# First batch of a block-sparse attention and Fourier-mixing kernel: two units' scores ahead of their two mask matmuls, masks on 64 rows, short steps of the second slot at once

## The chip, the cores and the metric

One core of a Trainium2 chip; the experiments ran on two chips, as said below. The metric is the time of one execution in microseconds (us), as the median of the runs quoted. All runs compared here are in the same, fast state; the one exception is named where it occurs. The clock records of a trace show what share of its full clock PE was granted, in stretches of 3.4 us or multiples of it (3.41, 6.83 and 17.07 us in the kernel before); a stretch at 0.50 is called a *half-clock window*.

The engines are written as the profile writes them: PE (TensorE, matmuls), PEld (its weight loads), DVE (VectorE), ACT (ScalarE), POOL (GpSimd), SP (the queue that starts transfers). Times inside an execution count from its first instruction.

## The reference

```python
# attention: q, k, v of (4, 8, 768, 64); blocks of 32 -> 24 x 24 blocks
scores = scale * np.matmul(q, k.transpose(0, 1, 3, 2))
# mask: band of width 1, first and last block row and column, 3 random blocks per row
scores = np.where(mask, scores, -1000000000.0)
scores = scores - np.max(scores, axis=-1, keepdims=True)
attn = np.exp(scores)
attn = attn / (np.sum(attn, axis=-1, keepdims=True) + 1e-09)
attn_out = np.matmul(attn, v)                 # -> x of (4, 768, 512)

# Fourier mixing and a channel MLP
X = np.fft.fft(np.fft.fft(x, axis=1), axis=2)
u = x + np.real(X).astype(np.float32)
un = (u - mean(u)) / np.sqrt(var(u) + 1e-06)
return u + np.maximum(un @ w_ch1, 0.0) @ w_ch2
```

## The kernel before

A *unit* is one block of 128 keys against 384 queries for two heads, a *slot* is two units, and a batch has 24 slots. In the first batch the mask is added to the scores by a second matmul into the same PSUM tile (written by PE's matmuls; the mask matmul has 24 rows: one for each block); from the second batch on the mask is instead multiplied in on DVE after the exponential. While the first batch runs, ACT and DVE also convert the MLP's weights, 32 *weight rounds* of two ACT and five DVE instructions.

```python
at_k = acc_p.tile([P, 2, 2 * HS], BF16, tag="acc", name="at_k")   # mask operands, bf16
at_q = acc_p.tile([P, 2, 2 * HS], BF16, tag="acc", name="at_q")
of_k, off_q, keep_q = at_k[:, 0, :], at_q[:, 0, :], at_q[:, 1, :]
# ... rows 0:24 and 64:88 are filled (D = 64, NB = 24, HS = 384)

def scores(u):                                    # one unit
    # ... (timing model left out)
    s = ps_s.tile([P, 2, 512], FP32, tag="s", name="s")
    for i in range(2):                            # 64 rows, f32
        nc.tensor.matmul(s[:, i, 0:HS], kT[D * i:D * i + D, c * P:(c + 1) * P],
                         qT[D * i:D * i + D, half * HS:(half + 1) * HS],
                         start=True, stop=n >= NP)
    if n < NP:                                    # first batch: 24 rows, bf16
        for i in range(2):
            nc.tensor.matmul(s[:, i, 0:HS], of_k[D * i:D * i + NB, c * P:(c + 1) * P],
                             off_q[D * i:D * i + NB, half * HS:(half + 1) * HS],
                             start=False, stop=True)
    return s

def w_round(i):                                   # one weight round
    nc.scalar.mul(out=lo.bitcast(FP32), in_=lo, mul=2.0 ** -52)
    nc.scalar.mul(out=a.bitcast(FP32), in_=hi.bitcast(FP32), mul=2.0 ** -112)
    # ... four DVE instructions on a and dst
    nc.vector.tensor_add(out=dst, in0=dst, in1=a.bitcast(FP32))

def slot(sl):
    for u, ps in [(u, scores(u)) for u in units]:
        weigh(u, ps)                              # exp on ACT (second batch: then mask on DVE)
    # ... values of the slot before (o), sums (sp)
    if sl == 1:
        short.append(("t", 0.0, lambda: turn(0, 0, 1)))   # transpose second half of first q
    # ...
    while short and (s in (2, 5) or len(short) > 1 or phase == 0 or r == 0):
        ready = [i for i in short if max(i[1], min(free[i[0]])) <= when["PE"] + 0.1]
        if not ready and s not in (2, 5) and r > 0:
            break                                 # short step left for the next slot
        # ... do one short step
    # ...
    w_steps(sl)                                   # weight rounds due by this slot
```

## Time and profile before

| | before |
|---|---|
| median of 3 runs | 1109.58 us (1108.61 to 1111.27) |
| PE busy | 1065.3 us, 96% of the profiled span |
| first scores of batch 1, of batch 2 | 8.60, 135.41 us |
| scores with their masks, per slot (start to start) | 2.23 us |
| longest wait of PE in batch 1 | 4.04 us, ended at 25.27 by the copies of q on DVE |
| first masked multiply of batch 2 (DVE) | 140.19 us |

A busy PE shows that PE is the engine to save time on; it does not show that every saving arrives. So the rows to look at are those where PE hands over to another engine: the wait at 25.27, and the start of the second batch, where its work waits for DVE. A timeline line reads: start, duration, engine, source line, operation, output <- inputs, shapes, count, and in brackets the idle time before it with what ended it. The prediction shows the lines.

### The profile page before, as it was taken

How to read it: one execution, taken by the hardware profiler on the slowest of the kernel's cores; microseconds unless marked ns; L12 is line 12 of the kernel's file. 1: busy time of each engine (PE TensorE's matmuls, PEld its weight loads, DVE VectorE, ACT ScalarE, POOL GpSimd, SP SyncE). 2: the span in 40 equal slices, each digit the busy share in tenths (PEclk: the TensorE clock that was granted, in tenths of full speed). 3: DMA queues.
4: the chain of work that ended last, by engine and by line, in shares of the span. 5: the costliest groups of instructions: out<-in, count | busy, mean ns of one | idle time of the engine just before them, and what ended most of it. 6: DMA issues, size and time to landing. Idle time of an engine off the chain costs nothing.

```text
span 1108.8 us, 12273 instructions
## 1 busy us (share of the span) xinstructions
PE 1065.3 (96%) x4370; PEld 537.9 (49%) x4370; DVE 670.6 (60%) x1227; ACT 389.8 (35%) x786; POOL 271.2 (24%) x302
## 2 busy tenths in 40 slices
PE   7999988998899999999999999999999999999996
PEld 4333333443455545444444545444444555568675
DVE  5688878497864535564558635555456446575563
ACT  5788755565202102253443212344330202120210
POOL 1000078487200001245537000343540000000000
PEclk9999999999999999999999999999999999999998
DMA  7557322022000000212210000211000000100001
GB/s 237 151 161 234 109 53 59 15 44 43 1 1 1 1 1 19 62 24 39 43 29 15 0 1 1 55 46 29 1 1 1 0 1 20 38 1 1 1 16 44
DMA packets 86689, 44.28 MB, mean 40 GB/s; under 512 B 74318, under 2 KB 79452, under 8 KB 86620
## 3 DMA queue, kind: packets, MB, share of 16 engines
q1 hardware_dynamic: 84732, 42.62, 14.5%
q10 hardware_dynamic: 1856, 0.79, 0.3%
q8 instruction: 36, 0.59, 0.2%
q14 instruction: 33, 0.27, 0.1%
q0 software_dynamic: 32, 0.01, 0.0%
HBM read 37.11 MB, written 6.29 MB: 39 GB/s over the span
## 4 chain that ended last, share of the span: by engine, by line
PE 83%; DVE 10%; ACT 2%; issue 2%; DMA 1%; POOL 1%; SPq 0%; ACTq 0%; DVEq 0%; POOLq 0%
PE y L1017 23%; PE z L961 14%; PE s L541 10%; PE o L585 8%; PE yp L961 7%; PE yy L1080 6%; PE xp L961 3%; DVE e L562 3%; PE zp L774 1%; PE sp L632 1%; PE zp L745 1%; DMA out_dram<-x 1%; PE xt L603 1%; PE tp L483 1%; DVE w_sb L452 1%
## 5 line engine op out<-in xcount | busy, mean ns | idle before, releaser
L572 POOL TENSOR_TENSOR acc<-acc,e 128x384 f32<-128x384 f32 x192 | 197.4, 1060 | 89.5 <-DVE e L562 88.9
L541 PE MATMUL s<-qT,kT 64*128 64x384 f32 x768 | 164.4, 531 | 15.2 <-DVE e L562 11.0
L562 DVE TENSOR_TENSOR e<-s,mask 128x768 f32<-128x768 f32 x144 | 131.1, 949 | 65.0 <-ACT s L560 62.9
L585 PE MATMUL o<-e,vr 128*64 128x384 f32 x768 | 148.0, 507 | 0.0
L560 ACT ACTIVATE s<-s 128x768 f32<-128x768 f32 x144 | 109.5, 791 | 89.3 <-PE s L541 88.1
L1020 DVE TENSOR_TENSOR x<-y,x 128x512 f32<-128x512 f32 x72 | 49.8, 691 | 146.8 <-PE y L1017 146.7
L1017 PE MATMUL y<-w_sb,hA 128*128 128x512 f32 x288 | 129.5, 595 | 1.1 <-ACT zs L776 1.1
L1017 PE MATMUL y<-w_sb,hB 128*128 128x512 f32 x288 | 128.5, 596 | 1.0 <-DVE x L1020 1.0
L572 POOL TENSOR_TENSOR acc<-e 128x384 f32<-128x384 f32 x48 | 50.0, 1063 | 231.3 <-DVE e L562 189.1
L541 PEld LDWEIGHTS s<-qT,kT 64*128 64x128 f32 x768 | 62.4, 187 | 85.1 <-DVE e L562 37.9
L966 DVE TENSOR_TENSOR hA<-z,hA 128x384 f32<-128x384 f32 x64 | 35.7, 558 | 97.5 <-PE z L961 97.5
L961 PE MATMUL z<-unT,t 128*128 128x384 f32 x256 | 93.0, 486 | 0.0
L837 POOL TENSOR_SCALAR st<-st 128x1 f32<-128x1 f32 x24 | 6.7, 277 | 348.1 <-DVE st L836 347.7
L1017 PEld LDWEIGHTS y<-w_sb,hB 128*128 128x128 f32 x288 | 53.3, 190 | 67.3 <-issue 65.6
L585 PEld LDWEIGHTS o<-e,vr 128*64 128x64 f32 x768 | 47.4, 138 | 75.9 <-issue 72.3
L1017 PEld LDWEIGHTS y<-w_sb,hA 128*128 128x128 f32 x288 | 52.9, 190 | 62.9 <-issue 58.5
L970 ACT ACTIVATE hA<-hA 128x384 f32<-128x384 f32 x64 | 33.5, 523 | 119.9 <-DVE hA L966 119.5
L961 PEld LDWEIGHTS z<-unT,t 128*128 128x128 f32 x256 | 48.6, 190 | 33.9
L970 ACT ACTIVATE hB<-hB 128x384 f32<-128x384 f32 x64 | 33.5, 523 | 86.1 <-DVE hB L966 86.1
L961 PE MATMUL xp<-unT,w_sb 128*128 128x384 f32 x128 | 48.5, 503 | 1.3 <-DVE x L1020 0.7
L981 ACT COPY hA<-xp 128x384 f32<-128x384 f32 x32 | 15.3, 479 | 95.8 <-PE xp L961 95.8
L961 PE MATMUL z<-t,w_sb 128*128 128x384 f32 x128 | 46.6, 487 | 0.9 <-DVE t L923 0.9
(197 smaller groups left out, 1409.1 us busy)
## 6 DMA issues: line engine op xcount, KB each, us to landing
wraw<-in_moe_w_ch_dram SPq DMA_DIRECT2D x32, 512.0 KB
vr<-in_v_dram SPq DMA_DIRECT2D x30, 192.0 KB
qr<-in_q_dram SPq DMA_DIRECT2D x48, 64.0 KB
kr<-in_k_dram SPq DMA_DIRECT2D x14, 192.0 KB
qb<-in_q_dram SPq DMA_DIRECT2D x28, 96.0 KB
kb<-in_k_dram SPq DMA_DIRECT2D x28, 96.0 KB
out_dram<-x SPq DMA_DIRECT2D x16, 128.0 KB
out_dram<-x SPq DMA_DIRECT2D x8, 256.0 KB
```

Of the source, the lines that this page charges most:

```text
L541: nc.tensor.matmul(s[:, i, 0:HS], kT[D * i:D * i + D, c * P:(c + 1) * P], qT[D * i:D * i + D, half * HS:(half + 1) * HS], start=True, stop ...
L560: nc.scalar.activation(out=s[:, :, 0:HS], in_=s[:, :, 0:HS], func=ACT.Exp, scale=scale)
L562: nc.vector.tensor_tensor(out=e, in0=s[:, :, 0:HS], in1=m.broadcast_to([P, 2, HS]), op=ALU.mult)
L572: nc.gpsimd.tensor_add(out=acc, in0=e_of[u - 1][:, i, :] if c == 1 else acc, in1=e[:, i, :])
L585: nc.tensor.matmul(o[D * i:D * i + D, :], vt[:, i, c, :], e[:, i, :], start=(c == 0), stop=(c == C - 1))
L961: nc.tensor.matmul(to, a[:, k, :], c[:, k, :], start=(k == 0), stop=(k == ND // 2 - 1))
L966: tt(out=to, in0=ps, in1=a, op=ALU.add)
L970: nc.scalar.activation(out=h, in_=h, func=ACT.Relu)
L981: nc.scalar.copy(out=h11, in_=x)
L1017: nc.tensor.matmul(y, hs[0, half][:, l, m * P:(m + 1) * P], w2_sb[:, 4 * r + l, :], start=(l == 0), stop=(l == 3))
L1020: nc.vector.tensor_tensor(out=x[:, m, :], in0=y, in1=x[:, m, :], op=ALU.add)
L1080: nc.tensor.matmul(ps, a[:, k, :], c[k // 2][:, k % 2, :] if isinstance(c, list) else c[:, k, :], start=(k == 0), stop=(k == 3))
```

## The change

Two things were meant to be saved in the first batch: changes of shape on PE between the scores (64 rows) and the masks (24 rows), by doing both units' scores first and giving the masks 64 rows as well, with zeros in the unused ones; and the 4 us wait, by doing the second transposes of the first q in slot 1 instead of leaving them for slot 2.

```diff
+    nc.vector.memset(of_k, 0.0)
+    nc.vector.memset(off_q, 0.0)
...
-    def scores(u):
+    def scores(us):
...
+        for u in us:                       # both units' scores
...
+            for i in range(2):
+                rows = slice(D * i, D * i + D)
+                nc.tensor.matmul(s[:, i, 0:HS], kT[rows, c * P:(c + 1) * P], qT[rows, queries],
+                                 start=True, stop=n >= NP)
+        for u, s in got if n < NP else ():  # then both units' masks, 64 rows
...
+                rows = slice(D * i, D * i + D)
+                nc.tensor.matmul(s[:, i, 0:HS], of_k[rows, c * P:(c + 1) * P], off_q[rows, queries],
                                  start=False, stop=True)
-        return s
+        return got
...
-            for u, ps in [(u, scores(u)) for u in units]:
+            for u, ps in scores(units):
...
-            if not ready and s not in (2, 5) and r > 0:
+            if not ready and s not in (2, 5) and r > 0 and sl > 1:
                 break
```

More of the change, by code (lines that the diff above doesn't have):

```diff
@@ L531 @@
     SLOT = 2
-    def scores(u):
-        n, w = divmod(u, UP)
-        half, c = divmod(w, C)
+    def scores(us):
+        n, w = divmod(us[0], UP)
+        half = w // C
         qT, kT = turned[n, 0], turned[n, 1]
-        s = ps_s.tile([P, 2, 512], FP32, tag="s", name="s")
-        busy("PE", 0.72 if n >= NP else 1.0, max(e_at.get(u - SLOT, 0.0), z_at[u % 2]))
-        s_at[u] = when["PE"] + HOP
-        for i in range(2):
-            nc.tensor.matmul(s[:, i, 0:HS], kT[D * i:D * i + D, c * P:(c + 1) * P],
-                             qT[D * i:D * i + D, half * HS:(half + 1) * HS],
-                             start=True, stop=n >= NP)
-        if n < NP:
-            for i in range(2):
-                nc.tensor.matmul(s[:, i, 0:HS], of_k[D * i:D * i + NB, c * P:(c + 1) * P],
-                                 off_q[D * i:D * i + NB, half * HS:(half + 1) * HS],
+        queries = slice(half * HS, (half + 1) * HS)
+        got = []
+        for u in us:
+            c = u % C
+            s = ps_s.tile([P, 2, 512], FP32, tag="s", name="s")
+            got.append((u, s))
+            busy("PE", 0.72, max(e_at.get(u - SLOT, 0.0), z_at[u % 2]))
+            s_at[u] = when["PE"] + HOP
+            for i in range(2):
+                rows = slice(D * i, D * i + D)
+                nc.tensor.matmul(s[:, i, 0:HS], kT[rows, c * P:(c + 1) * P], qT[rows, queries],
+                                 start=True, stop=n >= NP)
+        for u, s in got if n < NP else ():
+            c = u % C
+            busy("PE", 0.25)
+            s_at[u] = when["PE"] + HOP
+            for i in range(2):
+                rows = slice(D * i, D * i + D)
+                nc.tensor.matmul(s[:, i, 0:HS], of_k[rows, c * P:(c + 1) * P], off_q[rows, queries],
                                  start=False, stop=True)
-        return s
+        return got
     def weigh(u, s):
```

## The prediction

By *drain* it means the 0.21 us that scores take more ahead of another shape (0.85 against 0.64 us); the trace shows that time, not what PE does in it. For half clock behind a rest of PE it had the one gap of 4.04 us to go by, at the end of which the clock fell to 0.50 (24.15 to 30.98 us). The 0.16 us for a first mask was not shown by that trace; the runs show it below.

> **What bounds the kernel now.** I read the page first: PE is busy 96% of the span and the chain that ended last is 83% PE. The change, though, touches only the units of the first batch, so I asked for busy time by stretch. I cut it at the first scores (8.60), at the slot after the one long gap (33), in the middle, at the first scores of the second batch (135.41, where the scores lose their mask matmuls) and at the start of the dense matmuls (290).
>
> ```profile
> core 0: us, PE busy (x) PEld busy (x) DVE busy (x) ACT busy (x) POOL busy (x), PEclk, DMA share, GB/s
> 8.60:33.00 24.40, 20.36 (x110) 7.04 (x109) 10.73 (x29) 13.88 (x28) 0.00 (x0) 0.86 0.81 247
> 33.00:80.00 47.00, 46.59 (x290) 16.45 (x288) 37.74 (x80) 39.09 (x81) 0.00 (x0) 1.00 0.48 150
> 80.00:135.40 55.40, 55.40 (x348) 19.69 (x347) 48.49 (x109) 44.97 (x92) 0.00 (x0) 1.00 0.60 183
> 135.40:290.00 154.60, 136.66 (x718) 60.96 (x718) 119.79 (x166) 83.23 (x173) 111.51 (x112) 0.97 0.17 39
> ```
>
> From 33 to 135 PE never rests: what PE saves there, the stage saves, until ACT (39.09/47 = 83%) or DVE (48.49/55.4 = 88%) takes over. In the first stretch 4 us of PE are empty and the clock is not full. The timeline of PE then shows one slot of the first batch (two units):
>
> ```profile
> 75.23 0.92 PE L541 MATMUL s<-qT,kT 64*128 64x384 f32 x4
> 76.08 0.34 PE L546 MATMUL s<-at_q,at_k 24*128 24x384 bf16 x2
> 76.34 0.92 PE L541 MATMUL s<-qT,kT 64*128 64x384 f32 x4
> 77.19 0.34 PE L546 MATMUL s<-at_q,at_k 24*128 24x384 bf16 x2
> 77.46 1.51 PE L585 MATMUL o<-e,vr 128*64 128x384 f32 x8
> 78.90 0.85 PE L632 MATMUL sp<-e,pick 128*32 128x384 f32 x8
> 79.68 0.33 PE L357 MATMUL m<-at_q,at_k 24*128 24x384 bf16 x1
> 79.94 0.92 PE L541 MATMUL s<-qT,kT 64*128 64x384 f32 x4
> ```
>
> Durations contain the pipeline, so I use start to start: scores 0.85, mask 0.26, scores 0.85, mask 0.27: 2.23 us for two units. The second batch has two units of scores side by side:
>
> ```profile
> 242.99 1.56 PE L541 MATMUL s<-qT,kT 64*128 64x384 f32 x8
> 244.48 0.55 PE L603 MATMUL xt<-ident,oT 128*128 128x128 f32 x3
> ```
>
> 1.49 us for two units, so 0.64 for scores followed by scores of the same shape, and 0.85 for scores followed by another shape. The second thing to see is the gap, in the timeline of all engines from 5 to 34:
>
> ```profile
> 15.75 0.66 PE L483 MATMUL tp<-ident,qk 128*128 128x128 f32 x4
> ...
> 16.44 1.03 ACT L492 COPY qT<-tp 128x128 f32<-128x128 f32 x6 [1.99 <-PE tp L483]
> ...
> 18.56 0.44 PE L483 MATMUL tp<-ident,qr 128*128 128x128 f32 x2
> ...
> 20.37 0.85 PE L632 MATMUL sp<-e,pick 128*32 128x384 f32 x8
> ...
> 24.57 0.55 DVE L492 COPY qT<-tp 128x128 f32<-128x128 f32 x3
> 25.27 1.65 PE L541 MATMUL s<-qT,kT 64*128 64x384 f32 x4 [4.04 <-DVE qT L492]
> ```
>
> The second half of the first q is transposed at 18.56, one slot late, and its DVE copies stand in program order behind two weight rounds (ten instructions, 18.61 to 24.57). PE waits 4.04 us, and then the same four matmuls take 1.65 instead of 0.92 us until 32.
>
> [...] 0.21 us more on leaving the scores' shape, none within it. [...]
>
> **The change part by part.**
> *Order of scores and masks.* Per slot: scores 0.64, scores, mask 0.16, mask 0.27. What the second scores take depends on whether f32 to bf16 on the same 64 rows still drains. If not, 0.64: sum 1.71, saving 0.52. If so, 0.85: sum 1.92, saving 0.31. No place in the trace has this passage. Going to 64 rows has no other purpose than avoiding it[...], so I give "no drain" 60% and count 0.43. There are 24 slots.
> *The two memsets*[...] lie on DVE before 8. The mask operand was ready at 7.97 (7.62 + 0.35) and is now needed at 8.60 + 0.64 + 0.64 = 9.9 or later. Cost on the path: about none.
> *Short steps of slot 1 at once.* The first transposes come at 14.9 (two slots earlier by 0.43 each), take 0.6, and their six ACT copies 0.9 or 1.0. There is one bank of this kind, so PE now waits for them, about 1 us, does the second transposes at 16.6 and starts slot 2 at 17.0. DVE is idle then and copies at once, before the weight rounds. ACT, in order: square of q (0.9) to 17.9, the two weight rounds (2.3, read from 17.34 to 19.60) to 20.2, exps of slot 2 to 21.6. PE: 17.0 + 1.8 + 1.44 + 0.78 = 21.1 for slot 3, whose first score buffer is free at 20.9. So slot 3 runs almost without a wait and at full clock, and slot 4 starts at about 25.1 instead of 32.33: **7.2 us**, of which 0.9 to 1.3 belong to the new order in slots 0 to 3.
> *The other 20 slots:* 20 x 0.43 = 8.6. Against it: with one unit's scores directly behind the other's, the second score buffer is needed 0.48 us earlier (0.64 instead of 1.11 to 1.12 behind the first). In heavy ACT slots (two weight rounds, copies, a square) the exps end only just in time: at 64.6 for scores at 64.21 and 65.33. I take five such slots at 0.3: minus 1.5. PE would enter the second batch 7.2 + 8.6 - 1.5 = **14.3 us** earlier.
>
> *DVE sets a second limit.* There the first masked multiply stands behind the last weight round.
>
> ```profile
> 62.08 0.43 DVE L450 TENSOR_SCALAR wraw<-wraw 128x512 uint32<-128x512 uint32 x1 [3.13 <-ACT wraw L449]
> ...
> 140.19 1.80 DVE L562 TENSOR_TENSOR e<-s,mask 128x768 f32<-128x768 f32 x2
> ```
>
> The scores of 135.41 are multiplied at 140.19 only. A round is 2.98 us start to start (18.61 to 21.59); 32 rounds are 95.4, the eight tables 5.2, seven sums 3.2: 103.8. From 18.6 with the waits seen (4.4, 0.3, 4.1, 3.1, 1.6, 1.4, 1.8 = 16.7) this gives 139.1, so it accounts for the 140.2. After the change the rounds start at about 19.1 (behind the square), but the early waits mostly go, since DVE falls behind from the start: I leave 3. So 19.1 + 103.8 + 3 = 126, **14 us** earlier. Both limits say 14; I take 13.
>
> *Afterwards* no instruction is added or removed. The second batch's first part waits for DVE with PE (88% busy), but the order of its work is set relative to its own slots, so it shifts whole. The new durations in the kernel's own timing model (1.94 instead of 2.0 per slot) can reorder a few steps later. Sum: 1109.6 - 13 = **1096.5 us**.
>
> **The rivals.**
> 1. *DVE or ACT takes over.* For: 88% and 83% busy, and DVE already comes last at 140. Against: the waits of DVE sum to 16.7 us, those of ACT between 32 and 135 to some 18, so both have that room. If bursts spoil half of it, the gain is 7: 1102.
> 2. *f32 to bf16 drains regardless of rows.* For: the trace never shows the passage. Then 24 x 0.12 goes missing against my mean: gain 10 to 11, 1099. In the other case PE gains 2 more, which DVE would probably eat as a longer wait at 140: 1095.
> 3. *The stall moves.* The new wait of slot 1 for the bank, or exps behind two weight rounds, could again empty a clock window. For: ACT is packed from 15 to 22. [...] It would cost 4 to 6 us: 1101.
> 4. *The second batch reshuffles.* Three half-clock windows of 3.4 us lie there (the clock records of the trace have them at 196, 254 and 281); shifted work can lose one or catch another (1.7 us each), and a reordered mixer step can cost or win about 3.
>
> **Range and chances.** Rivals 1 to 3 mostly take from 13, and 4 spreads both ways: 1090 to 1104. Two per cent would need a gain of over 22 us, more than both mechanisms hold (7.2 + 20 x 0.52 = 17.6), so it could only come by luck in the second batch: 4%. A loss of 2% has no mechanism: 1%.
>
> **What would show it.** Right: the mask group has 64 rows; from the first scores to what follows the masks 1.7 us (or 1.9, the drain); the transposes of qr directly behind those of qk with about 1 us of PE wait for ACT before them; no wait of 4 us near 21 and no half clock before 190; first scores of the second batch near 121, first masked multiply near 126; the rest shifted by that amount. Wrong: a slot still at 2.2 us, PE waiting for the exps in most slots, or a gain at 140 that is lost again by 290.

## The result, and the profile after

| | before | after |
|---|---|---|
| median (range), 4 runs each, same rounds | 1110.09 (1108.61 to 1111.27) | 1100.71 (1098.54 to 1100.97) |
| profiled span | 1108.8 | 1099.1 |
| scores with masks, per slot | 2.23 | 1.81 |
| fifth slot can start (sums of the fourth done) | 32.33 | 26.64 |
| first scores of batch 2 | 135.41 | 123.32 |
| scores behind the first masked multiply | 141.18 | 129.84 |

A ratio here is the mean time of one kernel's fast runs over that of the other's in the same rounds, so not quite the ratio of the medians quoted. After over before is 0.9912 (0.9894 to 0.993): 9.4 us by the medians, within 2%. Predicted were 13 us, with a range of 5.6 to 19.6.

Busy time by stretch of the kernel after (columns as in the prediction's first fence):

```profile
26.64:70.00 43.36, 42.38 (x285) 17.16 (x281) 38.81 (x76) 38.63 (x80) 0.00 (x0) 1.00 0.60 177
70.00:123.32 53.32, 52.56 (x361) 20.92 (x357) 49.95 (x117) 46.58 (x95) 0.00 (x0) 1.00 0.66 206
```

PE still fills the first batch, but no longer wholly: 42.38 of 43.36 and 52.56 of 53.32. DVE rose to 94% of the second stretch. In before both stretches together had 0.41 us of PE idle; here it is 1.74.

The start of PE's work in the kernel after, from the timeline:

```profile
10.61 0.49 PE L559 MATMUL s<-at_q,at_k 64*128 64x384 bf16 x4
...
11.87 0.92 PE L551 MATMUL s<-qT,kT 64*128 64x384 f32 x4 [0.29 <-ACT e L569]
...
18.11 0.44 PE L486 MATMUL tp<-ident,qr 128*128 128x128 f32 x2 [1.12 <-ACT qT L495]
18.48 1.56 PE L551 MATMUL s<-qT,kT 64*128 64x384 f32 x8
19.87 0.49 PE L559 MATMUL s<-at_q,at_k 64*128 64x384 bf16 x4
20.29 1.51 PE L597 MATMUL o<-e,vr 128*64 128x384 f32 x8
```

The masks have 64 rows, and four of them stand together. From 18.48 to 20.29 are 1.81 us for what took 2.23. The transposes of qr now wait 1.12 us for ACT's copies, and the 4.04 us wait is gone. The cost of the order is in the second line: slot 1's scores wait for an exponential. ACT's first exponentials, before:

```profile
9.85 0.81 ACT L557 ACTIVATE e<-s 128x768 f32<-128x768 f32 x1 [1.78 <-PE s L546]
```

and after:

```profile
11.01 1.51 ACT L569 ACTIVATE e<-s 128x768 f32<-128x768 f32 x2 [2.94 <-PE s L559]
```

The first starts 1.16 us later, 0.54 more than the later first scores (9.22 against 8.60) explain, because it now stands behind both units' masks. And DVE's first weight round in the kernel after:

```profile
20.68 0.43 DVE L453 TENSOR_SCALAR wraw<-wraw 128x512 uint32<-128x512 uint32 x1 [1.54 <-ACT wraw L452]
```

It starts at 20.68, not at the predicted 19.1. The entry to the second batch, before:

```profile
141.18 1.78 PE L541 MATMUL s<-qT,kT 64*128 64x384 f32 x8 [1.51 <-DVE e L562]
```

and after:

```profile
129.84 2.00 PE L551 MATMUL s<-qT,kT 64*128 64x384 f32 x8 [2.26 <-DVE e L574]
131.77 2.83 PE L597 MATMUL o<-e,vr 128*64 128x384 f32 x8
```

PE waits longer for DVE, 2.26 instead of 1.51 us, and then the eight value matmuls take 2.83 instead of 1.51: the clock has halved (0.50 from 131.28). From here on I call these scores, the first that wait for a masked multiply, the *gated scores*.

To find where time goes after that, I matched the two traces matmul by matmul and took how much earlier each one starts than in before. Points are given in before's time; the clock records of each trace give the stretches at half clock.

| before's time | 134 | 141.5 | 149.5 | 156 | 282 | 302 | 736 | 745 | end |
|---|---|---|---|---|---|---|---|---|---|
| after is earlier by | 12.1 | 11.3 | 9.8 | 8.6 | 8.6 | 8.2 | 8.1 | 9.8 | 9.8 |
| after, run again | 13.0 | 12.2 | 10.8 | 10.6 | 10.6 | 10.1 | 9.8 | 11.5 | 11.5 |

Of the 12.1 us at the head of batch 2, 0.8 go in the longer wait for DVE, 2.7 in two half-clock windows (131.3 and 141.5) that before does not have, 0.4 around before's 282 to 302, where after has two half-clock windows in a row and before one, and 0.1 up to 736; 1.6 come back at 737.5 to 740.9, where before has a half-clock window and after has none. Nothing else moves: from the second batch on the order of instructions is the same in both kernels on every engine.

The windows around the gated scores (columns as before; PEclk is the third number from the right), after:

```profile
127.90:131.30 3.40, 1.46 (x8) 0.60 (x8) 3.18 (x7) 0.69 (x2) 0.57 (x1) 1.00 0.34 112
131.30:134.70 3.40, 3.40 (x11) 0.95 (x10) 1.92 (x2) 1.09 (x2) 3.34 (x5) 0.50 0.00 0
```

and of before, cut where its own half-clock windows would fall (those later in its trace follow each other on one grid of 3.4 us: 194.82, 252.84, 280.15 and 737.54 lie 17, 8 and 134 steps of 3.41 apart):

```profile
140.20:143.60 3.40, 2.42 (x14) 0.95 (x16) 2.88 (x5) 1.39 (x2) 1.52 (x2) 1.00 0.27 85
```

In after, a window in which PE works 1.46 of 3.40 us is followed by one at clock 0.50. In before the rest is spread over two windows (2.87 and 2.42 us busy) and the clock stays at 1.00.

### The profile page after: what moved, and what is told of

Same layout as the page of the kernel before. It is cut to its first block, busy times and chain, and to the rows that moved or that the text cites. A ratio compares the mean times of both kernels' runs of the same rounds, so it can differ in the third digit from the quotient of the medians.

```text
span 1099.1 us, 12275 instructions
## 1 busy us (share of the span) xinstructions
PE 1057.1 (96%) x4370; PEld 540.9 (49%) x4370; DVE 670.6 (61%) x1229; ACT 390.1 (35%) x786; POOL 271.2 (25%) x302
## 4 chain that ended last, share of the span: by engine, by line
PE 83%; DVE 9%; issue 2%; ACT 2%; DMA 1%; POOL 1%; SPq 0%; DVEq 0%; ACTq 0%; POOLq 0%
PE y L1029 23%; PE z L973 15%; PE s L551 10%; PE o L597 8%; PE yp L973 7%; PE yy L1092 6%; PE xp L973 4%; DVE e L574 3%; PE zp L786 2%; PE zp L757 1%; DMA out_dram<-x 1%; PE sp L644 1%; PE xt L615 1%; PE utp L898 1%; PE tp L486 1%
## 5 line engine op out<-in xcount | busy, mean ns | idle before, releaser
L551 PE MATMUL s<-qT,kT 64*128 64x384 f32 x768 | 158.3, 526 | 13.1 <-DVE e L574 11.5
L1029 PE MATMUL y<-w_sb,hB 128*128 128x512 f32 x288 | 128.5, 596 | 1.0 <-DVE x L1032 1.0
L973 PE MATMUL yp<-unT,w_sb 128*128 128x384 f32 x128 | 48.0, 499 | 0.4 <-DVE un L822 0.4
```

The costliest lines, as they stand in the source:

```text
L551: nc.tensor.matmul(s[:, i, 0:HS], kT[rows, c * P:(c + 1) * P], qT[rows, queries], start=True, stop=n >= NP)
L973: nc.tensor.matmul(to, a[:, k, :], c[:, k, :], start=(k == 0), stop=(k == ND // 2 - 1))
L1029: nc.tensor.matmul(y, hs[0, half][:, l, m * P:(m + 1) * P], w2_sb[:, 4 * r + l, :], start=(l == 0), stop=(l == 3))
```

## The experiments

Twelve kernels were run. The first eight ran on one chip, the last four on another; each is compared with runs of the kernel before on the same chip (medians 1109.18 to 1109.4 on the first, 1110.56 on the second). All gave a correct result and all came within 2% of before.

My first theory was that the two parts overlap: each alone gains about 7 us, both together 9.4, because DVE limits the sum. The rival was that they simply add.

### The short-step edit alone

```diff
 # on the kernel before
-            if not ready and s not in (2, 5) and r > 0:
+            if not ready and s not in (2, 5) and r > 0 and sl > 1:
```

> The kernel before with only the last edit (all short steps of the second slot at once; scores and masks interleaved on 24 rows as before). My theory: the wait of 4 us near 21 and the half clock to 31 go, the fifth slot starts near 26.7 instead of 32.3, the second batch's first scores come near 130, and DVE (weight rounds done near 128.5 to 129) is then no longer late, so the scores of the slot after also lose their wait of 1.5 us: gain about 7, 1103 us. So this edit alone gives most of the whole gain of 9.4. Rival A (the stall only moves to the wait for the bank and for the exps): fifth slot near 31, 1109 us. Rival B (gains add up: 5.7 from this edit and the rest from the order): 1104.5, with the wait in the slot after still there.

Measured: 1103.14 us (1102.55 to 1106.16, 6 runs), ratio 0.9951 (0.9934 to 0.9968). The gated scores in its timeline:

```profile
134.75 1.78 PE L541 MATMUL s<-qT,kT 64*128 64x384 f32 x8 [1.51 <-DVE e L562]
```

The wait of 1.51 us is the same as in before, to the digit: DVE moved along with PE. So the picture of DVE as a second limit at a time of its own is wrong. The trace is 6.4 us earlier than before at this point, 5.9 if both are counted from their own first scores. The time is the 1103 us that I expected, but by luck: the wait that was to vanish is still there, and this profile has no half-clock window near 131 or 141.

### The order and the rows alone

```diff
 # on the kernel after
-            if not ready and s not in (2, 5) and r > 0 and sl > 1:
+            if not ready and s not in (2, 5) and r > 0:
```

> The changed kernel without its last edit (both units' scores, then both masks on 64 rows; short steps of the second slot as before). My theory: the gap near 21 and the half clock stay, the fifth slot starts near 32; each slot takes 1.81 instead of 2.23 for scores and masks; the second batch's first scores come near 128.5 to 129, and DVE still has about 10 of its 16.7 us of waits to give, so its last round ends near 132; gain about 7, 1103 us. This edit and the last one then each give about 7 alone but 9.4 together, because DVE limits the sum. Rival (gains add up): 9.4 less what the last edit gives alone, so 2.5 to 4 us, 1106 to 1107.5.

Measured: 1104.32 us (1102.76 to 1105.76, 6 runs), ratio 0.9949 (0.9934 to 0.9965). The early wait is back:

```profile
25.98 2.93 PE L551 MATMUL s<-qT,kT 64*128 64x384 f32 x8 [4.46 <-DVE qT L495]
```

Counted from the first scores, the gated scores are earlier than in before by 5.9 with the edit alone, 6.8 with order and rows alone, and 12.0 with both. So in the first batch the two **add** (5.9 + 6.8 = 12.7), and the first theory falls. In the times, 6.3 and 5.1 us (of medians 1109.4) against 9.4 look as if something were lost, but by the profiles the difference comes behind the first batch, in the half-clock windows.

### Order kept, masks on 24 rows

```diff
 # on the kernel after, in the mask matmuls
-                rows = slice(D * i, D * i + D)
+                rows = slice(D * i, D * i + NB)
```

> The changed kernel with the mask matmuls on 24 rows again (order and short steps as changed, the instruction order of every engine the same). Scores, scores, masks, masks should take 1.91 instead of 1.81 us per slot, because the passage from scores to masks then changes the shape as well as the type (0.85 instead of 0.75 for the second scores). My theory (DVE sets the start of the second batch): its first scores come about 2 us later, near 125.5, but the first masked multiply stays near 129, and the time stays within 1 us of the changed kernel, 1101. Rival (PE sets it): 2.4 us slower, 1103.

Measured: 1098.85 us (1098.27 to 1101.09, 5 runs), ratio 0.9909 (0.9892 to 0.9926). One slot:

```profile
109.85 1.56 PE L551 MATMUL s<-qT,kT 64*128 64x384 f32 x8
111.34 0.50 PE L559 MATMUL s<-at_q,at_k 24*128 24x384 bf16 x4
111.77 1.51 PE L597 MATMUL o<-e,vr 128*64 128x384 f32 x8
```

1.92 us per slot instead of 1.81: PE loses 0.11 a slot on the change from 64 to 24 rows, and counted from the first scores batch 2 starts 1.7 us later than in after (115.79 against 114.10 us). (The rows themselves cost no time: four masks take 0.50 us on 24 rows and 0.49 on 64.) The gated scores follow by 1.5 us, although DVE has exactly the same work. So DVE's limit is not fixed: its rounds wait for ACT, for 5.3 us in all here against 4.0 in after, and ACT's work is given out slot by slot at PE's pace. The time is no longer than after's; in the profiles this run's clock grid fell differently, and none of the windows near 131 and 141 went to half clock. A 1.5 us effect was thus hidden by one of 2.7.

### Masks on 64 rows, order as before

```diff
 # on the kernel after: each unit's masks directly behind its scores
         for u in us:
             # ... two score matmuls
+            if n < NP:
+                for i in range(2):
+                    rows = slice(D * i, D * i + D)
+                    nc.tensor.matmul(s[:, i, 0:HS], of_k[rows, ...], off_q[rows, queries],
+                                     start=False, stop=True)
-        for u, s in got if n < NP else ():
-            # ... two mask matmuls
```

> The changed kernel with scores and masks interleaved again, but the masks on 64 rows. If passing from f32 to bf16 and back costs about 0.11 us each way within one shape, a slot's scores and masks take 0.75 + 0.27 + 0.75 + 0.26 = 2.03 us; if only the way to bf16 costs, 1.92; if rows alone mattered, 1.71. The first exp of a slot starts earlier than in the changed kernel. My theory (DVE sets the start of the second batch): first scores near 127 to 128, first masked multiply near 129 to 130, time 1101 to 1102.5. Rival (PE sets it): 3 to 5 us slower than the changed kernel, 1104 to 1106.

Measured: 1097.52 us (1097.14 to 1099.27, 4 runs), ratio 0.9895 (0.9876 to 0.9914). One slot:

```profile
116.78 0.92 PE L551 MATMUL s<-qT,kT 64*128 64x384 f32 x4
117.52 0.33 PE L558 MATMUL s<-at_q,at_k 64*128 64x384 bf16 x2
117.69 0.81 PE L551 MATMUL s<-qT,kT 64*128 64x384 f32 x4
118.33 0.33 PE L558 MATMUL s<-at_q,at_k 64*128 64x384 bf16 x2
118.59 1.51 PE L596 MATMUL o<-e,vr 128*64 128x384 f32 x8
```

1.81 us, exactly as with the new order, and none of the three sums that I had expected; the time, too, is below both ranges. On 64 rows the passage between f32 and bf16 costs nothing (0.64 for the second scores, 0.17 for the first masks). So the **rows alone give the whole saving of 0.42**; the order alone gives 0.31 (1.92 on 24 rows, the run before), and nothing more once the rows are 64. It then only delays the first exponential: counted from their first scores, the gated scores come 0.85 us earlier here than in after (119.77 against 120.62 us), in one profile each. These slots come out as a sum of three terms: 0.64 for two heads' scores and 0.16 for their masks; 0.10 whenever PE leaves a shape (the last masks take 0.26 above); 0.11 whenever f32 weights of 128 columns enter in a new shape (the first scores take 0.74 above, and 0.75 in other slots).

| order | leaves | f32 entries | sum | measured |
|---|---|---|---|---|
| s m s m, 24 rows (before) | 4 | 2 | 1.60 + 0.40 + 0.22 = 2.22 | 2.23 |
| s s m m, 24 rows | 2 | 1 | 1.60 + 0.20 + 0.11 = 1.91 | 1.92 |
| s s m m, 64 rows (after) | 1 | 1 | 1.60 + 0.10 + 0.11 = 1.81 | 1.81 |
| s m s m, 64 rows | 1 | 1 | 1.81 | 1.81 |

The entry of 0.11 us may be the load of the weights: the trace's own records of these loads (PEld) last 182 to 187 ns in f32 and 94 in bf16 in after. If the load is the cause, starting a slot with the bf16 masks should be cheaper, which the next kernel tries.

### The change again, and masks first

The kernel after was run once more beside three new ones, since half-clock windows made single profiles hard to compare.

```diff
 # after_again: the kernel after, unchanged
 # masks first: as in the run before, with the masks ahead of the scores
         for u in us:
             s = ps_s.tile([P, 2, 512], FP32, tag="s", name="s")
+            # two mask matmuls on 64 rows, start=True, stop=False (first batch)
             # two score matmuls
-                                 start=True, stop=n >= NP)
+                                 start=n >= NP, stop=True)
```

> The changed kernel once more, beside the three below. Time within 1.5 us of 1100.7. What I look at is whether the half-clock windows lie at the same places: if they depend on where the clock's windows of 3.4 us fall against the kernel's waits, those at 131 and 141 may be gone or moved, while those near 186, 244 and 271, which every run so far had, stay.

> Interleaved again and on 64 rows, but the mask matmuls of a unit before its scores. Theory from the interleaved run on 64 rows (0.75 + 0.16 + 0.64 + 0.26 per slot): each change of shape costs 0.10 on leaving and, with f32 weights of 128 columns, 0.11 on entering; the passage between f32 and bf16 costs nothing. Then a slot that enters with the bf16 mask should save the 0.11: 0.16 + 0.64 + 0.16 + 0.74 = 1.70 us, 24 x 0.11 = 2.6 us of PE less than interleaved 64 rows. Rival (entering costs 0.11 whatever the weights): 1.81 as there. Time: PE enters the second batch 2 us earlier than in the interleaved run, where DVE and ACT already press, so 1096 to 1098 against 1100.7 for the changed kernel.

Measured: after again 1098.95 us (1098.74 to 1100.81, 5 runs), ratio 0.9913 (0.99 to 0.9926), the first result repeated (its median 1.75 us lower, a little more than I had allowed); masks first 1096.87 us (1094.81 to 1098.68, 5 runs), ratio 0.9886 (0.987 to 0.9902). A slot with the masks first:

```profile
116.85 0.34 PE L554 MATMUL s<-at_q,at_k 64*128 64x384 bf16 x2
117.03 0.81 PE L558 MATMUL s<-qT,kT 64*128 64x384 f32 x4
...
118.57 1.51 PE L596 MATMUL o<-e,vr 128*64 128x384 f32 x8
```

1.72 us, against 1.70 by the sum without an f32 entry. The entry theory holds: the bf16 masks that enter take 0.18 instead of 0.16, and the scores that leave 0.74 instead of 0.64. Entering is 0.09 cheaper with bf16 than with f32, as much as the recorded loads differ; that the load is the cause fits this, but is not shown. In the time, the intervals of the two kernels overlap slightly; part of the saving is eaten at the gated scores, where PE's wait for DVE is 2.51 us.

Running the same kernel again also shows the clock's luck. The window before the gated scores, and that at them:

```profile
126.00:129.40 3.40, 1.10 (x11) 0.61 (x7) 3.30 (x8) 0.48 (x1) 0.00 (x0) 1.00 0.62 180
129.40:132.90 3.50, 3.50 (x14) 1.19 (x12) 2.34 (x4) 1.59 (x2) 2.69 (x3) 0.51 0.00 0
```

One half-clock window instead of two: with the same instructions in the same order, the second rest came to lie with 1.83 us of PE work in a window (136.3 to 139.7) instead of 1.42 (138.1 to 141.5 of the first profile).

### The weight rounds' last addition on GpSimd

```diff
 # on the kernel after
-        nc.vector.tensor_add(out=dst, in0=dst, in1=a.bitcast(FP32))
+        nc.gpsimd.tensor_add(out=dst, in0=dst, in1=a.bitcast(FP32))
```

> The changed kernel with the last of the five DVE instructions of each weight round (an f32 add, 0.73 us start to start) on GpSimd, which is idle in the first batch. Theory (DVE is late at the start of the second batch): DVE has 23 us less to do, the first masked multiply follows its exps at once, from first scores to the next slot's scores 5 us instead of 6.5, and the PE wait of 2.26 us there falls under 1: gain 1.5 us over the changed kernel, plus the half-clock windows it may avoid: 1097 to 1099. Rival (DVE only waits for ACT, which PE paces; or the GpSimd adds slow DVE down): the first masked multiply stays 5.5 us behind the first scores, no gain.

Measured: 1105.06 us (5 of 6 runs 1104.0 to 1105.7), ratio 0.996 (0.9947 to 0.9973). The sixth run took 6106 us and was marked slow, at full clock; I have no explanation for it. This was a **miss**: the kernel is slower than after. DVE's timeline:

```profile
64.45 1.29 DVE L453 TENSOR_SCALAR wraw<-wraw 128x512 uint32<-128x512 uint32 x1 [0.36 <-ACT wraw L452]
...
68.02 1.65 DVE L455 SCALAR_TENSOR_TENSOR w_sb<-wraw 128x512 uint32<-128x512 uint32 x1
```

These take 0.43 and 0.69 us in before. The two starts lie within GpSimd's additions (64.17 to 65.45 and 67.73 to 69.12), and the two DVE operations end 0.29 and 0.55 us after them, as if most of each had run only then. What held them is not shown. The mean of the L455 operation is 1199 ns here against 693. So the 0.7 us taken off DVE per round came back as waiting, and the gated scores wait 5.10 us. It says nothing for or against DVE as the limit.

### The waits of the second batch filled with idle matmuls

```diff
 # on the kernel after; warm(k) issues k matmuls whose result nobody reads
+        if n == NP + 1 and a == 0:
+            warm(3 + half)                       # beside the transposes of q
...
+            if b == 0 and half == 1 and m == 1:
+                warm(12)                         # before a mixer step
...
+        fill = {SB + 1: 8, SB + 13: 9, 2 * SB: 8}.get(sl, 0)
+        if fill:
+            warm(fill)                           # ahead of that slot's scores
```

> The changed kernel with dummy matmuls on PE where it waits in the second batch: before the second slot's scores (8, about 1.8 us), before the two transposes of the next q (3 and 4), before the scores near 184 (9), near 243 (8), and before the last transposes near 271 (12). They feed nothing. Theory (a half-clock window comes when PE has rested for about half of a window of 3.4 us): the half-clock windows near 131, 141, 186, 244 and 271 go; each costs up to 1.7 us: gain 3 to 6 us, 1095 to 1098. Rival (the half-clock windows are chance or follow load, not rest): they stay, and the time is that of the changed kernel or up to 1 us longer.

Measured: 1094.69 us (1094.38 to 1095.62, 4 runs), ratio 0.9874 (0.9859 to 0.9889); the mean clock is 0.996 to 0.997 in every run, where after's is 0.988 to 0.992. From 125.0 to 138.6 us, around the gated scores, the trace has it at 1.00 throughout. At the gated scores:

```profile
129.25 1.78 PE L553 MATMUL s<-qT,kT 64*128 64x384 f32 x8 [0.48 <-DVE e L576]
```

The scores start no earlier than in the repeated run of after (129.25 against 128.96), so the fill takes nothing from the wait itself. But the kernel is 4.3 us faster than after in the same rounds, by adding matmuls. So rest of PE, and not the load, halves the clock there (1.00 with PE at work for 3.40 and 2.92 us in the two windows from 125.0 to 131.8; in after 0.50 behind a window with 1.46).

### The last addition dropped

```diff
 # on the kernel after
-        nc.vector.tensor_add(out=dst, in0=dst, in1=a.bitcast(FP32))
```

This drops the low half of each weight on purpose; the result still passed the comparison.

> The changed kernel with the last of the five DVE instructions of each weight round left out (an f32 add; its result is then less exact on purpose, or counts as wrong), nothing put in its place: DVE has 23 us less to do and GpSimd stays out of it, unlike in the run before, where GpSimd slowed DVE's other instructions. Theory (DVE sets the start of the second batch): the first masked multiply comes right after its exps (these end near 126 in the changed kernel's trace), the PE wait of 2.26 to 2.30 us before the next slot's scores falls to under 0.5, and with it the half-clock window near 129 to 131 goes: 1.5 to 4 us faster than the changed kernel, 1095 to 1097.5. Rival (ACT, which PE paces, sets it): the wait stays near 2.3.

Measured: 1093.79 us (1091.92 to 1096.02, 5 runs), ratio 0.9842 (0.9823 to 0.9861). The head of batch 2:

```profile
121.57 1.56 PE L550 MATMUL s<-qT,kT 64*128 64x384 f32 x8
...
125.76 1.56 PE L550 MATMUL s<-qT,kT 64*128 64x384 f32 x8
```

The second line has no wait. With DVE lighter, the gated scores come 15.4 us earlier than in before, against 12.2 in the repeated run of after. So DVE's weight rounds do set the start of batch 2, and 3.2 us lie there. ACT, the rival, does not hold it. Whole-kernel profiles differ by 3.1 us (14.57 against 11.47), but the ratios by 0.7%, nearly 8 us; they come from different chips and rounds. Part of it is the choice of profile: the profiled run is the slowest of its five, 2.2 us above their median, with a clock of 0.989 where the others have 0.993 to 0.995. What the rest is stays open.

### Two full versions with the fill, and the fill on before

```diff
 # masks first, 64 rows, short-step edit, fill {SB + 1: 9, SB + 13: 9, 2 * SB: 8}
 # masks on 64 rows in the old order, short-step edit, fill as above (8, 9, 8)
 # the kernel before with the fill alone (6, 9, 8)
```

> The version that should beat both: masks first and interleaved on 64 rows, the short steps of the second slot at once, and the dummy matmuls in the waits of the second batch (9 before the second slot's scores). The masks-first order gained 1 to 2 us of PE over the changed kernel at the start of the second batch, the fill 4.3: 1092 to 1093.5, with a clock of 0.996 or 0.997 in every run. If the masks-first gain only turns into waiting for DVE: 1094.5, the time of the changed kernel with the fill.

> Interleaved scores and masks on 64 rows with the fill, to be held against the changed kernel with the fill (1094.7), with the clock out of play. Theory (the reordering adds nothing on PE once the rows are 64, 1.81 us per slot either way, and delays the first exp of each slot, which cost the first slots 0.4 to 0.8 us): 0.5 to 1 us faster, 1093.7 to 1094.2. Rival (the reordering is worth something of its own): slower than 1094.7.

> The kernel before with the same fill in the second batch (6 before the second slot's scores, where its wait is 1.5). It still has the wait near 21 with its half clock to 31. The other half-clock windows go: 1104 to 1106. Held against the changed kernel with the fill (1094.7) this says what the change is worth with the clock of the second batch out of play: theory (as the traces add up, 12.0 at the start of the second batch's gated scores, from the first scores on, less 0.6 or so where the start of the clock differs): 10 to 12 us. Rival (the change only shifted the clock's luck): 6 or less.

| | median | runs | ratio |
|---|---|---|---|
| masks first, fill | 1093.78 (1093.11 to 1094.34) | 4 | 0.9849 (0.9828 to 0.9871) |
| old order, 64 rows, fill | 1094.72 (1092.83 to 1095.95) | 4 | 0.9851 (0.9828 to 0.9874) |
| before, fill | 1108.29 (1106.94 to 1110.55) | 22 | 0.9981 (0.9974 to 0.9988) |

The masks-first version with the fill is 16.8 us faster than before on the same chip (1110.56) and, with its interval, faster than after (0.9913, other rounds and another chip). It computes the full result. It cannot be told from the old order with fill, nor with certainty from after with fill (0.9874): the intervals overlap. So neither of the first two expectations is decided: both times fall between theory and rival or on the rival's edge. Nor did the fill bring the full clock: the runs' mean is 0.995 to 0.997 in the first two and 0.992 to 0.993 in the third, which still has the half clock behind its early wait (0.50 from 23.8 to 30.6).

The last row was to answer how much of the change the clock hid. It missed its expectation of 1104 to 1106: the fill gives before only 2.1 us by the ratio's 0.19%, and after 4.3. Dividing 0.9874 by 0.9981 gives 0.9893, so with the fill on both sides the change is worth about 1.07% or 11.9 us, against the 9.4 us measured without it. This divides ratios from two chips, so it carries the errors of both: about 0.9876 to 0.991, which overlaps the 0.9894 to 0.993 without the fill. So rival "luck", 6 us or less, is ruled out, but that the clock hid 2.5 us is not shown by the times. The estimate agrees with what the traces have at the gated scores, 11.3 and 12.2 us.

## Why the prediction was right, and where its sizes were off

The direction and the range held, and the mechanism is the one described: 1100.71 us, and 1098.95 in a second set, against 1096.5. By its steps:

- **Slot 1's transposes**, "7.2 us": 5.7 (32.33 less 26.64), or 6.3 counted from the first scores. The wait itself was as counted (1.12 us against about 1), and no wait near 21 is left. What is missing: the first scores start 0.62 us later, because the clock was released later at the start of this execution (the warming matmuls ahead of them go from 213 to 111 ns start to start at 8.4 us, in before at 7.1), which is not the change: in the repeated run all 14 come at the shorter step, in 1.73 us from 6.69 against 2.49 from 6.80, and the first scores start at 8.35; and slot 1's scores wait for an exponential that the new order delays, which I did not count.
- **The 20 later slots**, "20 x 0.43 = 8.6", minus 1.5: 6.4 (103.08 us before, 96.68 after). Per slot 0.42, right in size but for another reason. It was meant as a mean of 0.52 (no drain) and 0.31 (drain), and neither happened. The passage from f32 to bf16 is free, as the first branch had it (0.64 us for the second scores on 64 rows), but the branch took all of the 0.21 us between 0.64 and 0.85 as the cost of leaving. Half of it is entering, and one entry per slot stays. 20 x 0.42 less 6.4 leaves 2.0 for waits and small losses; the waits on ACT and DVE that the trace names are 1.5.
- **Order and rows** were priced as one. They are not: the rows alone give the whole 0.42, the order alone 0.31, and on top of the rows nothing (the runs on 24 rows and with the old order on 64). The sentence "going to 64 rows has no other purpose than avoiding it", the drain, was right about what matters: the rows. The 0.16 for a first mask is what the runs gave, too (0.16 with masks first, 117.67 to 117.83).
- **The limit at DVE**, "14 us": 11.3. The step that failed is its start, "19.1": the first round begins at 20.68 (0.62 of the difference is the later first scores), and the waits are 4.0, not 3. With these, 20.68 + 103.8 + 4.0 = 128.5 against 128.85 in the trace; the sum of 103.8 was sound. It was wrong, however, to treat this as a limit of its own beside PE: with the edit alone and with the masks on 24 rows it moved along with PE, since ACT feeds DVE at the pace of the slots. It does set the start of batch 2 (the run with the addition dropped), and so it seems in before too, whose trace has DVE without a wait from 123.2 to the first masked multiply at 140.19.
- **"It shifts whole" behind the gate** (the gated scores), with the clock left to chance (rival 4): this is half of where the point value failed. Of the 13 us, 11.3 were there at the gated scores, 1.7 short, and 9.7 at the end, another 1.6 short. Two half-clock windows at 131 and 141 took 2.7 us. They are not pure chance: the change made PE wait longer at the gate (2.26 us), long enough to empty more than half of one window (3.41 us). Where the windows fall against the work differs from run to run: in the repeated run PE's work is 0.9 us earlier (first scores of batch 2 at 122.40 against 123.32), the half-clock window 1.9 us (129.4 against 131.3), and only one comes. At before's 737 luck gave 1.6 back: PE worked 1.67 us in the window ahead of it in both kernels, and only before's was followed by half clock. And the idle window that the prediction read into the early stall was not wholly idle: from 20.80 to 24.20 PE worked 0.42 us in before, and the clock went to 0.50 all the same. The other half of rival 4, a new order of work in batch 2, did not happen.
- **The memsets**, "about none": right, 0.38 us each at 1.10 and 1.51 (recorded as 384 elements of uint32), when DVE had nothing else to do that anyone waited for.
- Rival 1 (DVE or ACT takes over) came true by a small part: some 1.5 us of waits in the slots and 0.8 at the gate. Rival 3 (a stall that moves) came true only as rest inside a window (PE at work for 1.46 and 1.42 of 3.40 us), not as an empty one.
- Two of the prediction's sums are a tenth off (17.0 + 1.8 + 1.44 + 0.78 is 21.0, and 1109.6 less 13 is 1096.6). Nothing rests on them.

So the sum is: 5.7 + 6.4 = 12.1 at batch 2, minus 0.8 at the gate, minus 2.7 and 0.4 at half clock and 0.1 of small losses, plus 1.6: 9.7, and the profiled spans differ by 9.7.

Open are: what rest in a window halves the clock exactly, since windows with equal PE work went both ways; what the entry into a shape consists of; why dropping the addition gains more in the times than in the trace; and the run of 6106 us.

## What to carry to other kernels

Price a change of tile shape on PE as two terms, leaving and entering (0.10 and 0.11 us here), and ask whether giving the small operand the same rows removes both; then the order of the matmuls can be chosen for the engine that waits for them. When two engines feed each other, a saving on one can move the other's "limit" too (with the short-step edit alone PE's wait for DVE stayed at 1.51 us), so test it by making that engine's work lighter rather than by adding up its instructions. And once PE has short waits, look at the rest in each clock window before judging a difference of one or two microseconds: cheap matmuls that fill the waits were worth 4.3 us here, beside 9.4 for the change under study.

## What the traces show of shapes and the clock

- A change of shape cost 0.10 us on leaving one, plus 0.11 on entering one with f32 weights of 128 columns and 0.02 with bf16 (0.18 against 0.16); changing between f32 and bf16 on the same 64 rows cost none (0.64 us for scores before masks as before scores).
- A window that is partly busy can be followed by half clock. Windows with PE at work for 1.10 (the repeated run), 1.42 and 1.46 of 3.40 us (after) were followed by one at 0.50, while windows with 1.80 (masks on 64 rows in the old order), 1.83 (the repeated run) and 2.42 us (before) were not. In between there is no sharp limit in these profiles, by modelled ends of the matmuls: 1.67 us was followed by half clock in before (734.1 to 737.5) and not in after (725.2 to 728.6). Behind a window already at half clock it went differently: after's window at 271.2, with PE at work for 2.52 us, was followed by a second one at half clock, before's at 280.2, with 2.91, was not.
- The run-to-run phase of the windows changes later stretches too: the same kernel had two half-clock windows near 131 to 145 us in one profile, which took 2.7 us, and one in another, which took 1.6.
- Matmuls without a use, put into short waits in the middle of the kernel, sped it up: 4.3 us of 1099 here, and 2.1 of 1110 for the kernel before.
